# Queries and keys split in place, a mixer chunk tied behind attention, a late copy moved, and a last tile's low half written across partitions

## The chip, the cores and the metric

The kernel runs on one core of a Trainium2 chip, in one launch. The metric is device time in microseconds (us). The engines are TensorE (PE, with its weight loads as PEld), VectorE (DVE), ScalarE (ACT), GpSimd (POOL) and SyncE (SP), which issues most of the DMAs. Every engine runs its own instructions strictly in the order in which they stand.

## The reference, cut to what matters

Three stages follow each other, all in float32: attention with 4 batches of 8 heads, then a token-shift mixture, then an MLP mixer.

```python
def _attn_ref(q, k, v, s):                      # q, k, v: (4, 8, 576, 64)
    scores = scale * np.matmul(q, k.transpose(0, 1, 3, 2))
    cum = np.cumsum(np.maximum(s, 0.0), axis=-1)
    bias = -(cum[:, :, :, None] - cum[:, :, None, :])
    scores = np.where(causal, -1e9, scores + np.minimum(bias, 0.0))
    scores = scores - np.max(scores, axis=-1, keepdims=True)
    attn = np.exp(scores)
    attn = attn / (np.sum(attn, axis=-1, keepdims=True) + 1e-09)
    return np.matmul(attn, v)

def _moe_ref(x, mu_k, mu_r, w_k, w_v, w_r):     # x: (4, 576, 512), d_ff 1024
    xk = mu_k * x + (1.0 - mu_k) * x_prev
    xr = mu_r * x + (1.0 - mu_r) * x_prev
    k = np.maximum(xk @ w_k, 0.0)
    v = k * k @ w_v
    r = 1.0 / (1.0 + np.exp(-(xr @ w_r)))
    return r * v

def _moe2_ref(x, w_tok1, w_tok2, w_ch1, w_ch2): # d_tok 256, d_ch 1536
    h = np.maximum(x.transpose(0, 2, 1) @ w_tok1, 0.0) @ w_tok2
    u = x + h.transpose(0, 2, 1)
    return u + np.maximum(u @ w_ch1, 0.0) @ w_ch2
```

## The kernel before

Float32 products are made of pairs: each operand is split into a high part (rounded to a shorter format, F32R) and a low part (the rest), and a product is high by high, high by low and low by high. `products` (line 108) is the helper through which all matmuls of the two later stages go.

**Attention.** The rows of batch 0 are done first, with simpler operands ("early" and "late" items). Batches 1 to 3 are 24 visits, one head each, `i` = 0 to 23. A visit has a tile of 128 queries per item `j` = 0 to 3; an even visit has a fifth item, `j` = 4, for the last 64 queries of its own head and of the next one together. That makes 108 items (`items`). An item is one chain: score matmuls (`scores`, lines 307 and 308), a maximum on DVE (278), an exponential on ACT (289), a sum on POOL (290), a reciprocal on DVE (291), a normalisation on POOL (292), and then transposes on PE (435) and the product with the values (493).

**The operands of a visit.** `X1[i % 2]` and `X2[i % 2]` are four tiles in all, so the tiles of visit `i` are free for visit `i + 2` when its last score matmul (the pair item's, for an even visit) has run. `x1` holds the bias rows and the high parts, `x2` the high and low parts crossed. Before the change they come from DRAM: `load` brings a quarter of the raw queries and keys of two heads into the tile `PB`; `split` (lines 238 to 240) makes the high part by a copy on ACT, the low part by a subtraction on POOL, and stores both to the DRAM tensor `hl_d`; `place` (266 to 269) later reads them back by three DMAs, and the bias rows by a fourth. All those DMAs are issued by SP.

**The mixture's work as filler.** `moe_units` cuts the mixture of a batch into units of 12 matmuls (`up` makes `h`, `gate` makes `r`, half a `down` makes `vd`), 20 units for each of its two column chunks (256 and 320 columns). These units are spread between attention items by the table `starts, ends` (792) and the loop behind it. The second chunk of batch 0 is spread from item `base + 1` on, where `base` is the first of the 108 items.

**What sets the order.** A scheduler at build time orders each engine's instructions by priority, set with `at(place)`, and by when it reckons that an instruction could start. The kernel's written order is thus not the engines' order; the rows in the section on the change show that.

**The late copy.** `late_pv` (423) ends with a DVE copy of a head pair's product into the mixture's input `xt`.

**The token stage.** `y_transpose` (853 to 860) makes `YN`, transposed rows in high and low parts; for the last tile of 64 rows the low part is made in the low half's own place and a DMA (860) copies it to partitions 64 to 127, behind the high part. `tok1` multiplies both at once (872, 873).

Of the kernel before, what the change touches and what calls it, by code (L numbers as in the profile page):

```python
# [19 lines left out]
def f32(ap):  # L20
    return ap.bitcast(F32)
# [3 lines left out]
def attention_moe_mixer(  # L25
# [189 lines left out]

    qk_raw = {}

    def stage():
        if "PB" not in act:
            act["PB"] = qk_p.tile([128, 8 * QC], F32, tag="HX", name="PB")  # L220
        return act["PB"]

    def part(y):
        x, c = divmod(y, 2)
        return x, S * c // 2, S * (c + 1) // 2

    def load(i, y):
        g = visits[i][0]
# [43 lines left out]

    def softmax_max(j, ps, P, mx, x, c0, c1, mask=None):
        q0 = 128 * j
        m = 128 if mask is not None else min(128, S - 128 * j)
        if mask is None:
            mask = maskc[:, 512 - q0 + c0:512 - q0 + c1]
        nc.vector.tensor_tensor_reduce(  # L278
            out=P[0:m, c0:c1], in0=ps[0:m, 0:c1 - c0], in1=mask[0:m],
            scale=-scale, scalar=3.0e38 if x == 0 else mx[0:m, x - 1:x],  # L280
            op0=ALU.add, op1=ALU.min, accum_out=mx[0:m, x:x + 1],
        )

# [10 lines left out]
    def scores(i, j):  # L294
# [7 lines left out]
        for x, (c0, c1) in enumerate(parts):  # L302
            ps = ps_s.tile([128, 512], F32, tag="s", name="s")
            for e in (1, 0) if pair else (0,):
                x1, x2 = xs(i + e)
                n, a = (TAIL * (1 + e), S - TAIL * (1 + e)) if pair else (128, q0)
                nc.tensor.matmul(ps[0:n, 0:c1 - c0], x1[:, 0, a:a + n], x1[:, 1, c0:c1], start=True, stop=False)
                nc.tensor.matmul(ps[0:n, 0:c1 - c0], x2[:, 0, a:a + n], x2[:, 1, c0:c1], start=False, stop=True)
            softmax_max(j, ps, P, mx, x, c0, c1, None if not pair else maskp if x else maskc[:, 0:c1])
        softmax(j, P, mx, x, pair)  # L310
        pst[i, j] = P

# [69 lines left out]
    def late(h, j):  # L382
# [28 lines left out]
    def late_pv(h):  # L411
# [233 lines left out]
    def attention_item(n):  # L645
        if n < N1:
# [7 lines left out]
            if h >= H - 4:  # L654
                x = 3 * (h - H + 4) + j - 2
                with at(N0 + n + 0.1):
                    if x >= 4 and x < 8:
                        split(0, x - 4)
                    if x in (2, 3, 4, 5):
                        load(0, x - 2)  # L660
                    if x == 8:
                        load_v(0)
                    if x in (10, 11):
                        load(2, x - 10)
# [19 lines left out]
        if j == 0 and i + 1 < len(visits):  # L684
            with at(N0 + n):
                place(i + 1)
        if i % 2 == 0:
            with at(N0 + n + 0.1):
                if j < 4 and i + 2 < len(visits):
                    split(i + 2, j)  # L690
                    if j < 2:
                        load(i + 2, 2 + j)
                if j == NS - 1 and i + 2 < len(visits):
                    load_v(i + 2)
        else:
            with at(N0 + n + 0.1):
                if 2 <= j < 4 and i + 3 < len(visits):
                    load(i + 3, j - 2)
            if j == 1 and i + 1 < len(visits):
                with at(N0 + n + 0.2):  # L700
                    split_v(i + 1)
# [150 lines left out]
    def y_transpose(b, h):  # L852
        for i in range(NS):
# [170 lines left out]
```

## Time and profile before

| | us |
|---|---|
| three timed runs | 877.49, 1112.56, 873.9 (median 877.49) |
| the profiled execution | 872.61 |
| its span, first to last instruction | 870.8 |

The granted TensorE clock of the profiled execution is 0.992 of full speed on the mean. PE is busy 840.6 us of the span, its weight loads 790.5 us, DVE 485.1, ACT 452.6 and POOL 343.4. One timed run is far above the other two and is left out of everything that follows. "Busy" of PE is drawn from matmuls that overlap each other, so a PE that is busy throughout can still be slower than it could be.

### The profile page before, as it was taken

Reading aid. Unit: us, or ns where it says so; the run is one execution under the profiler, and the core shown is the slowest. Engines: PE = TensorE matmul, PEld = TensorE weight load, DVE = VectorE, ACT = ScalarE, POOL = GpSimd, SP = SyncE. Lnnn points to the kernel's source line nnn. Section 1 sums busy time; section 2 is a strip of 40 time slices with the busy share of each in tenths; the row PEclk is TensorE's granted clock in tenths of the full one; section 3 lists DMA queues with packets and bytes.
Section 4 is the critical chain, followed back from the end, with each engine's and each line's share of the span. In section 5 each row is a group of like instructions: output and inputs, shape, how many; then the busy total and the mean of one; then the engine's idle time right before and its main releaser. Section 6 shows DMA issues by size and latency. Waiting matters only on the chain. (4 is left out here: it accounts for less than half of the span.)

```text
span 870.8 us, 17455 instructions
## 1 busy us (share of the span) xinstructions
PE 840.6 (97%) x6127; PEld 790.5 (91%) x6127; DVE 485.1 (56%) x1352; ACT 452.6 (52%) x1257; POOL 343.4 (39%) x601
## 2 busy tenths in 40 slices
PE   8889998999899999999999999999999999999998
PEld 5656777988789999999999989999999999999998
DVE  5797776565879566985469757951331222222221
ACT  4688766865886656868377865840310221211210
POOL 4565666864785544645256854720000000000000
PEclk9899999999999999999999999999999999999999
DMA  7943778687974244431234746553021112112100
GB/s 191 266 134 88 199 218 230 192 240 210 252 204 133 70 111 117 100 93 41 83 94 129 230 143 217 177 181 94 7 92 54 44 31 74 42 32 73 38 25 26
DMA packets 88024, 108.36 MB, mean 124 GB/s; under 512 B 11152, under 2 KB 71568, under 8 KB 87936
## 3 DMA queue, kind: packets, MB, share of 16 engines
q1 hardware_dynamic: 81408, 91.56, 37.7%
q0 software_dynamic: 4576, 15.08, 5.5%
q8 instruction: 49, 0.80, 0.4%
q10 hardware_dynamic: 1952, 0.60, 0.3%
q14 instruction: 39, 0.32, 0.1%
HBM read 77.74 MB, written 28.90 MB: 122 GB/s over the span
## 5 line engine op out<-in xcount | busy, mean ns | idle before, releaser
L863 ACT ACTIVATE HID<-c 128x256 fp32r<-128x256 f32 (+1 forms) x96 | 39.3, 410 | 220.9 <-PE c L108 220.8
L108 PE MATMUL vd<-KK,WV 128*128 128x256 f32 (+1 forms) x768 | 120.9, 300 | 0.1
L108 PEld LDWEIGHTS vd<-KK,WV 128*128 128x128 f32 x768 | 106.6, 188 | 2.4 <-issue 0.9
L292 POOL TENSOR_SCALAR P<-P,sum 128x128 f32<-128x128 f32 (+4 forms) x148 | 93.6, 636 | 36.2 <-DVE sum L291 30.2
L108 PE MATMUL h<-XK,WK 128*128 128x320 f32 (+1 forms) x672 | 105.9, 303 | 0.7 <-DVE XK L517 0.5
L108 PE MATMUL c<-HID,WV 128*128 128x256 f32 (+1 forms) x768 | 104.9, 291 | 0.0
L108 PE MATMUL c<-U,WK 128*128 128x256 f32 (+1 forms) x768 | 103.2, 291 | 1.4 <-DVE HID L864 1.4
L289 ACT ACTIVATE P<-P,mx 128x128 f32<-128x128 f32 (+4 forms) x148 | 86.9, 588 | 30.3 <-DVE mx L278 23.0
L108 PEld LDWEIGHTS c<-HID,WV 128*128 128x128 f32 x768 | 100.6, 188 | 0.0
L108 PEld LDWEIGHTS c<-U,WK 128*128 128x128 f32 x768 | 98.6, 188 | 1.7 <-DVE HID L864 1.7
L108 PEld LDWEIGHTS h<-XK,WK 128*128 128x128 f32 x672 | 93.8, 189 | 2.1 <-DVE XK L517 0.7
L864 DVE SCALAR_TENSOR_TENSOR HID<-c,HID 128x256 fp32r<-128x256 f32 (+1 forms) x96 | 43.8, 456 | 81.1 <-ACT HID L863 81.0
L278 DVE CUSTOM_DVE_ANT_0 P<-s,maskc 128x128 f32<-128x128 f32 (+4 forms) x148 | 69.1, 478 | 22.1 <-PE t L435 8.4
L928 DVE TENSOR_TENSOR ut<-c,ut 128x256 f32<-128x256 f32 (+1 forms) x32 | 14.6, 458 | 119.3 <-PE c L108 112.0
L529 POOL TENSOR_TENSOR KK<-k,KK 128x256 fp32r<-128x256 f32 (+1 forms) x64 | 55.8, 877 | 19.8 <-ACT k L528 18.7
L108 PE MATMUL r<-XR,WR 128*128 128x320 f32 (+1 forms) x384 | 60.0, 299 | 0.0
L290 POOL TENSOR_SCALAR sum<-sum 128x1 f32<-128x1 f32 (+1 forms) x148 | 32.4, 219 | 67.6 <-ACT P L289 57.2
L108 PE MATMUL c<-HID,WR 128*128 128x256 f32 (+1 forms) x384 | 54.8, 291 | 0.0
L108 PEld LDWEIGHTS r<-XR,WR 128*128 128x128 f32 x384 | 52.8, 188 | 1.1 <-ACT raw L614 0.4
L108 PE MATMUL c<-U,C1A 128*128 128x256 f32 (+1 forms) x384 | 52.8, 296 | 0.1
L108 PEld LDWEIGHTS c<-U,C1A 128*128 128x128 f32 x384 | 51.5, 190 | 0.3 <-ACT U L913 0.3
L108 PEld LDWEIGHTS c<-HID,WR 128*128 128x128 f32 x384 | 51.3, 188 | 0.0
(133 smaller groups left out, 1658.4 us busy)
## 6 DMA issues: line engine op xcount, KB each, us to landing
X<-hl_d SPq DMA_DIRECT2D x72, 288.0 KB
hl_d<-PB SPq DMA_DIRECT2D x48, 288.0 KB
raw<-in_moe_w_ch_dram POOLq DMA_DIRECT2D x48, 256.0 KB, 3.3
PB<-in_qk_dram SPq DMA_DIRECT2D x48, 144.0 KB
yt<-y_d SPq DMA_DIRECT2D x16, 288.0 KB
u_d<-yt SPq DMA_DIRECT2D x16, 288.0 KB
raw<-in_moe_w_k_dram SPq DMA_DIRECT2D x8, 512.0 KB
raw<-in_moe_w_v_dram SPq DMA_DIRECT2D x16, 256.0 KB
```

Of the source, the lines that this page charges most:

```text
L108: nc.tensor.matmul(ps, a, b, start=first and i == 0, stop=last and i == n - 1)
L278: nc.vector.tensor_tensor_reduce(out=P[0:m, c0:c1], in0=ps[0:m, 0:c1 - c0], in1=mask[0:m], scale=-scale, scalar=3.0e38 if x == 0 else mx[0 ...
L289: nc.scalar.activation(out=P[0:m, 0:w], in_=P[0:m, 0:w], func=AF.Exp, bias=mx[0:m, x:x + 1], scale=-1.0, accum_out=sm[0:m, 0:1])
L290: nc.gpsimd.tensor_scalar(out=sm[0:m, 0:1], in0=sm[0:m, 0:1], scalar1=1e-9, scalar2=1.0, op0=ALU.add, op1=ALU.mult)
L292: nc.gpsimd.tensor_scalar(out=P[0:m, 0:w], in0=P[0:m, 0:w], scalar1=sm[0:m, 1:2], scalar2=1.0, op0=ALU.mult, op1=ALU.mult)
L529: nc.gpsimd.tensor_tensor(out=kk[:, 1, m, 0:n], in0=t[:, 0:n], in1=f32(kk[:, 0, m, 0:n]), op=ALU.subtract)
L863: nc.scalar.activation(out=hi, in_=ps, func=AF.Relu)
L864: nc.vector.scalar_tensor_tensor(out=lo, in0=ps, scalar=0.0, in1=f32(hi), op0=ALU.max, op1=ALU.subtract)
L928: nc.vector.tensor_tensor(out=t, in0=ps, in1=t, op=ALU.add)
```

## The change

Four edits:

1. Queries and keys are loaded raw, a head at a time, into one half of the partitions of a tile `RQ` (even visits in partitions 0 to 63, odd ones in 64 to 127), two visits ahead. When the operand tiles come free, `place` makes the high part by two copies on ACT straight into `x1`, the low part by four subtractions on POOL straight into `x2`, and copies the high part from `x1` to `x2` by two DMAs within the chip's own memory. `hl_d` and its stores and reads are gone.
2. The units of batch 0's second mixture chunk are spread over items `base + 3` to `base + PER + 8` (before: `base + 1` to `base + PER + 2`; `PER` is 36), and each is tied: its PE instructions stand behind the last score matmul of the item at which it is planned (`heads`). Batch 1's 40 units start 6 items later and end where they did.
3. The last late copy is issued behind the maximum of visit 0's second item.
4. The low part of `YN`'s last tile is written by DVE across partitions, without the DMA.

```diff
-    hl_d = dram.tile([G - H, D, 4, S], F32, name="hl_d")
...
-    def split(i, y):
-        g = visits[i][0] - H
-        x, c0, c1 = part(y)
-        t = qk_raw.pop((i, y))
-        e = stage()[:, S + y % 2 * S:S + y % 2 * S + S].rearrange("p (t s) -> p t s", t=2)
-        copy("A", e[:, 1].bitcast(F32R), t)
-        nc.gpsimd.tensor_tensor(out=e[:, 0], in0=t, in1=e[:, 1], op=ALU.subtract)
-        nc.sync.dma_start(out=hl_d[g:g + 2, :, 2 * x:2 * x + 2, c0:c1].rearrange("h d t s -> (h d) t s"), in_=e)
+    def sides(i):
+        a, z = slice(0, D), slice(D, 2 * D)
+        return (a, z) if i % 2 == 0 else (z, a)
...
+    def load(i):
+        nc.sync.dma_start(out=raw_qk()[sides(i)[0]], in_=qk[visits[i][0]])
...
     def place(i):
         g = visits[i][0]
-        t = hl_d[g - H]
         if i < 2:
             X2[i] = x_tile(2 + i, F32R)
         x1, x2 = xs(i)
-        nc.sync.dma_start(out=f32(x1[0:4]), in_=ext_d[g])
-        nc.sync.dma_start(out=f32(x1[64:128]), in_=t[:, 1:4:2])
-        nc.sync.dma_start(out=f32(x2[0:64]), in_=t[:, 0:4:3])
-        nc.sync.dma_start(out=f32(x2[64:128]), in_=t[:, 1:3])
+        a, z = sides(i)
+        rq = raw_qk()[a]
+        nc.sync.dma_start(out=f32(x1[z][0:4]), in_=ext_d[g])
+        for y in (1, 0):
+            nc.scalar.activation(out=x1[a, y], in_=rq[:, y], func=AF.Copy)
+            high, low = (z, a) if y else (a, z)
+            nc.sync.dma_start(out=f32(x2[high, y]), in_=f32(x1[a, y]))
+            for c in range(2):
+                cs = slice(S * c // 2, S * (c + 1) // 2)
+                nc.gpsimd.tensor_tensor(out=x2[low, y, cs], in0=rq[:, y, cs], in1=f32(x1[a, y, cs]), op=ALU.subtract)
+        if i + 2 < len(visits):
+            load(i + 2)
...
+    def last_late_copy():
+        with tc.issue_after(maxima[-1]):
+            copy("D", xt[0, H // 2 - 1][:, 1 + QC:1 + S], late_ps[H // 2 - 1])
...
-    starts, ends = [0, 2, 4, 4], [2, 4, 4, 4]
+    starts, ends = [0, 8, 4, 4], [8, 4, 4, 4]
...
-                m = base + 1
+                m = base + 3
                 todo.setdefault(m + (x1 - m) * x // len(u1), []).append(acts)
-            x1 = base + 1
+                tied.add(id(acts))
+            x1 = base + 3
...
-            with at(N0 + n + 3):
+            with at(N0 + n + 3), tc.issue_after(heads[n - 0]) if id(acts) in tied else ExitStack():
                 run(acts)
...
-            nc.vector.tensor_tensor(out=YN[0:r, 1, i, :], in0=ps[0:r, :], in1=f32(YN[0:r, 0, i, :]), op=ALU.subtract)
-        nc.sync.dma_start(out=f32(YN[TAIL:2 * TAIL, 0, NS - 1, :]), in_=f32(YN[0:TAIL, 1, NS - 1, :]))
+            low = YN[:, 1, i, :] if r == 128 else YN[TAIL:2 * TAIL, 0, i, :]
+            nc.vector.tensor_tensor(out=low, in0=ps[0:r, :], in1=f32(YN[0:r, 0, i, :]), op=ALU.subtract)
```

**PE, from the last items of visit 7 to the first transposes of visit 8.** `s` are scores (`X_1469` and `X_1471` are `x1` of even and odd visits, `X_1576` and `X_1718` their `x2`), `t` transposes of a normalised tile, `pv` products with the values, `h` and `vd` units of the mixture. `P_2948` is the last tile of visit 7 and `P_2987` the first of visit 8. Before:

```order
L307 MATMUL s<-X_1469 64x288
L308 MATMUL s<-X_1576 64x288
L435 MATMUL t<-ident,P_2948 128x128 x4
L493 MATMUL pv<-PF,VV_1933 128x256 x2
L493 MATMUL pv<-PF,VV_1933 128x128 x2
L435 MATMUL t<-ident,P_2987 128x128
L307 MATMUL s<-X_1471 128x128
L308 MATMUL s<-X_1718 128x128
L307 MATMUL s<-X_1471 128x256
L308 MATMUL s<-X_1718 128x256
```

After the change, where the same two tiles are `P_2866` and `P_2925`, and the odd visits' `x1` and `x2` are `X_1445` and `X_1659`:

```order
L434 MATMUL t<-ident,P_2866 128x128 x4
L107 MATMUL h<-XK,WK 128x256 x3
L492 MATMUL pv<-PF,VV_1902 128x256 x2
L492 MATMUL pv<-PF,VV_1902 128x128 x2
L300 MATMUL s<-X_1445 128x288
L301 MATMUL s<-X_1659 128x288
L300 MATMUL s<-X_1443 64x288
L301 MATMUL s<-X_1538 64x288
L434 MATMUL t<-ident,P_2925 128x128
L434 MATMUL t<-ident,P_2938 128x128 x2
L300 MATMUL s<-X_1445 128x128
L301 MATMUL s<-X_1659 128x128
L107 MATMUL vd<-KK,WV 128x320 x12
```

What moved: before, no unit of the mixture stands between the scores of visit 8's last items and those of visit 9 (nor, further on, until visit 10's second item); now a unit stands between most of them.

**POOL, while visit 4 is under way.** `P` are normalisations, `sum` the sums before them. Before, `PB` are subtractions of `split` for later visits:

```order
L292 TENSOR_SCALAR P_2376<-P_2376,sum 128x128
L290 TENSOR_SCALAR sum<-sum 128x1
L239 TENSOR_TENSOR PB<-PB 128x288
L290 TENSOR_SCALAR sum<-sum 128x1
L292 TENSOR_SCALAR P_2393<-P_2393,sum 128x256
L292 TENSOR_SCALAR P_2435<-P_2435,sum 128x384
L239 TENSOR_TENSOR PB<-PB 128x288
```

After, where `P_2342`, `P_2383` and `P_2400` are visit 4's tiles, and `X_1538` is `x2` of the even visits, being refilled for visit 6:

```order
L285 TENSOR_SCALAR P_2342<-P_2342,sum 128x256
L283 TENSOR_SCALAR sum<-sum 128x1
L285 TENSOR_SCALAR P_2383<-P_2383,sum 128x384
L283 TENSOR_SCALAR sum<-sum 128x1
L260 TENSOR_TENSOR X_1538<-RQ,X_1443 64x288 x3
L285 TENSOR_SCALAR P_2400<-P_2400,sum 128x512
L260 TENSOR_TENSOR X_1538<-RQ,X_1443 64x288
```

What moved: single subtractions scattered among the normalisations, done whenever their data were there, became four in a bunch, at the moment when the operand tile comes free.

## Rows read from the trace of the kernel before

**Rows 1.** The page: span, busy time, and weight loads in 40 slices.

```profile
span 870.8 us, 17455 instructions
...
PE 840.6 (97%) x6127; PEld 790.5 (91%) x6127; DVE 485.1 (56%) x1352; ACT 452.6 (52%) x1257; POOL 343.4 (39%) x601
...
PEld 5656777988789999999999989999999999999998
```

**Rows 2.** Windows of the attention stage: length, then engines' busy time, clock, DMA share.

```profile
137.00:150.00 13.00, 10.58 (x64) 8.75 (x63) 8.33 (x31) 8.81 (x26) 9.90 (x20) 0.93 0.92 239
150.00:214.00 64.00, 61.72 (x434) 59.49 (x433) 39.27 (x133) 45.80 (x128) 43.00 (x79) 0.99 0.78 216
214.00:262.00 48.00, 41.41 (x299) 37.03 (x298) 36.78 (x118) 38.73 (x115) 36.02 (x66) 1.00 0.82 225
262.00:300.00 38.00, 37.92 (x293) 36.89 (x292) 29.78 (x92) 26.14 (x72) 21.13 (x42) 1.00 0.40 111
300.00:437.00 137.00, 137.00 (x1036) 135.90 (x1034) 90.82 (x284) 89.30 (x242) 63.72 (x120) 1.00 0.35 91
```

**Rows 3.** Waits between 137 and 275 us: in total, times, longest.

```profile
ACT PB L75 <- DMA PB<-in_qk_dram: 22.8, 17, 3.6
POOL PB L239 <- ACT PB L75: 16.5, 12, 3.2
...
PE s L308 <- DMA X<-hl_d: 4.1, 3, 2.3
```

**Rows 4.** Timeline of ACT from 215 us.

```profile
216.08 0.45 ACT L75 ACTIVATE PB<-PB 128x288 fp32r<-128x288 f32 x1 [3.56 <-DMA PB<-in_qk_dram]
```

**Rows 5.** Timeline of PE from 224 us.

```profile
227.40 0.66 PE L493 MATMUL pv<-PF,VV 128*128 128x256 f32 x4
229.40 0.33 PE L435 MATMUL t<-ident,P 128*128 128x128 f32 x1 [1.34 <-POOL P L292]
```

**Rows 6.** Waits of PE between 150 and 214 us, the longest.

```profile
PE s L308 <- DMA X<-hl_d: 1.2, 1, 1.2
```

**Rows 7.** Groups of ACT by form: count, busy us, mean ns.

```profile
L289 ACT ACTIVATE P<-P,mx 128x576 f32<-128x576 f32 x12 | 9.3, 773 | 4.9 <-DVE mx L278 4.7
...
L289 ACT ACTIVATE P<-P,mx 64x576 f32<-64x576 f32 x8 | 6.3, 787 | 0.9 <-DVE sum L291 0.9
...
L75 ACT ACTIVATE PB<-PB 128x288 fp32r<-128x288 f32 x48 | 21.2, 441 | 30.7 <-DMA PB<-in_qk_dram 29.8 <-POOL PB L239 0.3 <-issue 0.2
...
L463 ACT ACTIVATE PT<-t 128x512 fp32r<-128x512 f32 x24 | 14.2, 594 | 0.5 <-PE t L435 0.2
```

**Rows 8.** Groups of POOL by form.

```profile
L239 POOL TENSOR_TENSOR PB<-PB 128x288 f32<-128x288 f32 x48 | 40.0, 835 | 23.9 <-ACT PB L75 18.6 <-DMA y_d<-e 3.7 <-DVE sum L291 0.6
...
L529 POOL TENSOR_TENSOR KK<-k,KK 128x320 fp32r<-128x320 f32 x32 | 29.4, 923 | 14.0 <-ACT k L528 13.8
...
L292 POOL TENSOR_SCALAR P<-P,sum 128x512 f32<-128x512 f32 x32 | 26.2, 820 | 12.6 <-DVE sum L291 11.0 <-PE t L435 1.0 <-PE h L108 0.4
```

**Rows 9.** Timeline of PE from 138 us: start, length.

```profile
138.20 0.29 PE L308 MATMUL s<-X 128*64 128x288 f32 x1
...
147.07 0.30 PE L308 MATMUL s<-X 128*128 128x128 f32 x1 [2.31 <-DMA X<-hl_d]
```

**Rows 10.** Timeline of SP from 139 us.

```profile
141.13 0.60 SPq L269 DMA_DIRECT2D X<-hl_d  x1
```

**Rows 11.** Timeline of PE from 470 us, a stretch without waits.

```profile
470.48 3.34 PE L108 MATMUL vd<-KK,WV 128*128 128x256 f32 x28
473.66 0.96 PE L108 MATMUL t<-T,H 128*128 128x288 f32 x6
...
476.24 3.68 PE L108 MATMUL h<-XK,WK 128*128 128x320 f32 x24
479.76 1.75 PE L108 MATMUL t<-T,H 128*128 128x288 f32 x12
```

**Rows 12.** The subtraction's line: shortest, median, longest in ns, first and last start.

```profile
L239 POOL TENSOR_TENSOR PB<-PB x48: 788/810/1083, 91.3 to 267.4; 128x288 f32<-128x288 f32 x48
```

**Rows 13.** PE's waits from 437 to 600 us.

```profile
PE c L108 <- DVE HID L864: 1.4, 1, 1.4
PE t L108 <- DVE yt L883: 1.2, 2, 1.0
PE t L872 <- DMA YN<-YN: 1.1, 1, 1.1
```

More of the change, by code (lines that the diff above doesn't have):

```diff
@@ L142, in attention_moe_mixer @@
     X1, X2, PT, VV = {}, {}, {}, {}
+    heads, maxima = [], []
     xt = {}
@@ L214, in xs, with raw_qk @@
         return X1[i % 2], X2[i % 2]
[L216 to L228, printed above, removed]
-        x, c0, c1 = part(y)
-        t = qk_raw[i, y] = stage()[:, y % 2 * S // 2:(y % 2 + 1) * S // 2]
-        nc.sync.dma_start(out=t, in_=qk[g:g + 2, :, x, c0:c1].rearrange("h d s -> (h d) s"))
-    def split(i, y):
-        g = visits[i][0] - H
-        x, c0, c1 = part(y)
-        t = qk_raw.pop((i, y))
-        e = stage()[:, S + y % 2 * S:S + y % 2 * S + S].rearrange("p (t s) -> p t s", t=2)
-        copy("A", e[:, 1].bitcast(F32R), t)
-        nc.gpsimd.tensor_tensor(out=e[:, 0], in0=t, in1=e[:, 1], op=ALU.subtract)
-        nc.sync.dma_start(out=hl_d[g:g + 2, :, 2 * x:2 * x + 2, c0:c1].rearrange("h d t s -> (h d) t s"), in_=e)
+    def sides(i):
+        a, z = slice(0, D), slice(D, 2 * D)
+        return (a, z) if i % 2 == 0 else (z, a)
+    def raw_qk():
+        if "RQ" not in act:
+            act["RQ"] = qk_p.tile([128, 8 * QC], F32, tag="HX", name="RQ")
+        return act["RQ"][:, 0:2 * S].rearrange("p (t s) -> p t s", t=2)
+    def load(i):
+        nc.sync.dma_start(out=raw_qk()[sides(i)[0]], in_=qk[visits[i][0]])
     def load_v(i):
@@ L277, in softmax_max @@
             mask = maskc[:, 512 - q0 + c0:512 - q0 + c1]
-        nc.vector.tensor_tensor_reduce(
+        maxima.append(nc.vector.tensor_tensor_reduce(
             out=P[0:m, c0:c1], in0=ps[0:m, 0:c1 - c0], in1=mask[0:m],
@@ L281, in softmax_max @@
             op0=ALU.add, op1=ALU.min, accum_out=mx[0:m, x:x + 1],
-        )
+        ).ins)
     def softmax(j, P, mx, x, pair=False):
@@ L307, in scores @@
                 nc.tensor.matmul(ps[0:n, 0:c1 - c0], x1[:, 0, a:a + n], x1[:, 1, c0:c1], start=True, stop=False)
-                nc.tensor.matmul(ps[0:n, 0:c1 - c0], x2[:, 0, a:a + n], x2[:, 1, c0:c1], start=False, stop=True)
+                mm = nc.tensor.matmul(ps[0:n, 0:c1 - c0], x2[:, 0, a:a + n], x2[:, 1, c0:c1], start=False, stop=True)
             softmax_max(j, ps, P, mx, x, c0, c1, None if not pair else maskp if x else maskc[:, 0:c1])
         softmax(j, P, mx, x, pair)
+        heads.append(mm.ins)
         pst[i, j] = P
@@ L391, in late @@
             ps = ps_s.tile([128, 512], F32, tag="s", name="s")
-            nc.tensor.matmul(ps[0:m, 0:c1 - c0], x[0:D + 4, 0, q0:q0 + m], x[0:D + 4, 1, c0:c1], start=True, stop=True)
+            mm = nc.tensor.matmul(ps[0:m, 0:c1 - c0], x[0:D + 4, 0, q0:q0 + m], x[0:D + 4, 1, c0:c1], start=True, stop=True)
             softmax_max(j, ps, P, mx, y, c0, c1)
+        heads.append(mm.ins)
         softmax(j, P, mx, y)
@@ L421, in late_pv @@
             nc.tensor.matmul(pv[rs, o:CM], late_v[p][0:r, k, rs], T[0:r, BLK[k] + o:BLK[k] + CM], start=k == 0, stop=k == NS - 1)
-        if e == 1:
+        if e == 1 and h < H - 1:
             copy("D", xt[0, p][:, 1 + QC:1 + S], pv)
+    def last_late_copy():
+        with tc.issue_after(maxima[-1]):
+            copy("D", xt[0, H // 2 - 1][:, 1 + QC:1 + S], late_ps[H // 2 - 1])
     def transposes(i, j):
@@ L653, in attention_item @@
                     late_values(h // 2 + 1)
-            if h >= H - 4:
-                x = 3 * (h - H + 4) + j - 2
+            if h == H - 3 and j == 2:
                 with at(N0 + n + 0.1):
[L657 to L664, printed above, removed]
+                    load(0)
+                    load(1)
+            if h == H - 2 and j == 4:
+                with at(N0 + n + 0.1):
+                    load_v(0)
             if h == H - 1 and j == 3:
@@ L686, in attention_item @@
                 place(i + 1)
-        if i % 2 == 0:
+        if i % 2 == 0 and j == NS - 1 and i + 2 < len(visits):
             with at(N0 + n + 0.1):
[L689 to L701, printed above, removed]
+                load_v(i + 2)
+        if i % 2 and j == 1 and i + 1 < len(visits):
+            with at(N0 + n + 0.2):
+                split_v(i + 1)
         with at(N0 + n):
             scores(i, j)
+        if (i, j) == (0, 1):
+            with at(N0 + n - 0.5):
+                last_late_copy()
         with at(N0 + n + 1.5):
@@ L791, in attention_moe_mixer @@
     base = (NS - 2) * H
-    starts, ends = [0, 2, 4, 4], [2, 4, 4, 4]
+    starts, ends = [0, 8, 4, 4], [8, 4, 4, 4]
+    tied = set()
     for b in range(B):
```

2 lines of the change are left out of this document (1 added, 1 removed).

## Prediction

> **What bounds the kernel now.** I read the page first: PE is busy 840.6 of 870.8 us, so nothing but its own waits can be won, and the slices of its weight loads show where these are, ahead of slice 14 or so of 40 [rows 1]. The first 100 us hold many of them, but the order on PE up to there is the same after the change. Then I read the windows of the attention stage [rows 2]. From 300 to 437 us weight loads run 135.90 of 137 us: 1.1 us lost, 0.8%. From 137 to 262 us they run 8.75 of 13, 59.49 of 64 and 37.03 of 48 us: 4.25, 4.51 and 10.97, together 19.73 us lost; from 262 to 300 it is 1.11. Next the waits of that stretch. Only 4.1 us of PE's own are on a DMA of the operands [rows 3]. More telling is ACT: 17 times the copy of `split` at the head of its queue waits for a raw quarter still on its way, 22.8 us in all, and everything behind it waits along. One of these, 3.56 us up to 216.08 [rows 4], lies at the start of the poorest stretch. The first transpose of visit 8 then finds its tile not ready and PE stands 1.34 us at 229.40 [rows 5], with no unit of the mixture in between, as the order shows: units were run as soon as PE had room, and are used up where the chains come late.
>
> **A rule on how to count.** By PE's matmul row the loss from 137 to 262 us is 2.42 + 2.28 + 6.59 = 11.3 us, by the weight loads 19.7 [rows 2]. The matmul counts side with the second: 299 in 48 us against 1036 in 137 is 160 ns against 132 each, and 299 at 132 ns would be 39.5 us, 8.5 less than they took, where the matmul row shows 6.6 idle. The Trainium skill ("Trainium Kernel Development and Optimization", Performance Expectations) says that matmul busy time is a bad metric because matmuls are pipelined, and that the busy share of the weight loads is a good one. By the matmul row the ceiling of the first term below would be 8.4 us lower.
>
> **The change part by part.**
>
> *The round trip through DRAM goes.* 48 stores to `hl_d`, 72 reads from it and 48 quarter loads leave SP's queue; 24 loads and 48 short copies come. The raw head is now loaded two visits ahead, so ACT's 22.8 us of waits for it [rows 3] go. ACT's and POOL's own work grows: per visit two copies of 64x576 and four subtractions of 64x288 stand for two and two of 128x288. Half the partitions save nothing: the exponential takes 787 ns on 64 partitions and 773 on 128 [rows 7]. A copy of 576 columns is not in the trace; from below 594 ns (512 columns), from above 787 ns; I take 0.66, since 128x512 is the nearest and 288 to 512 columns cost 441 to 594 ns, 0.7 ns a column [rows 7]. A subtraction is 0.835 us [rows 8], so a visit has 1.3 us of ACT (0.9 before) and 3.3 us of POOL (1.7 before).
>
> *What that costs while PE waits for it.* The refill of `x1` and `x2` starts when the tile's last score matmul has run. Its chain is: ACT finishes what it holds (0 to 3 instructions, about 0.6 us each), 0.66 copy, four subtractions 3.3, and on POOL one or two strangers in between, a normalisation 0.82 and a unit's subtraction 0.92 [rows 8]. That is 4.0 us at least, 7.5 at most without a wait, and I take 7.0, since the order shows such strangers within the bunch. The two copies by DMA run beside the subtractions. Before, the same path (free at 138.49 and used at 147.07 [rows 9], last read issued at 141.13 [rows 10]) took 8.6 us with the DMA engines 92% taken [rows 2]. How long PE has other work meanwhile I count in the new order and price at 0.114 us for a matmul of 256 columns (28 from 470.48 to 473.66) and 0.147 for 320 (24 from 476.24 to 479.76) [rows 11], 0.11 for a transpose: for the even visits 2 to 22 it is 6.3, 8.9, 6.7, 8.4, 6.7, 5.9, 8.9, 7.8, 8.3, 6.0 and 10.9 us; odd visits have 7.6 and more. For visit 6 that is 24 units' matmuls 3.5, nine value products 1.1, six transposes 0.7 and eight score matmuls of 128 to 512 columns 1.3. A chain of 7.0 us comes late by 0.7 + 0.3 + 0.3 + 1.1 + 1.0 = **+3.4 us**. At 4.0 us it is 0, at 9 us 16.
>
> *The tie and the new spread.* It adds and removes no work; it holds 20 units back so that one stands behind each second item or so. Priced as above, the work on PE between an item's scores and its transposes was 5.0 to 9.2 us in visits 7 and 8; in the new order the same items have 9.8 to 12.3, and the poorest afterwards is 5.9. What remains then? The stretch 150 to 214 us has such filler now, with POOL at 67% and ACT at 72%; without its wait for operands (1.2 us [rows 6]) it loses 3.3 of 64 us, 5.2% [rows 2]. At 5.2% the 125 us from 137 lose 6.5 instead of 19.7: **-13.2 us**. At the 0.8% of 300 to 437 it would be -18.7; if only half comes back, -7. The 2.31 us stop at 147 was followed by a slower clock, 0.93 of full over 13 us and 0.99 over 64 [rows 2]: 0.9 + 0.6 = **-1.5 us** if the stop goes; if it does not, 0.
>
> *The price of moving load.* `split` was done by 268 us for all visits [rows 12], so the stretch from 300 to 437 us had none of it. Now 11 visits there add 36 us to POOL's 63.7 of 137 (73%) and 14 to ACT's 89.3 (76%), and batch 1's units are squeezed into 32 items from 38. That is a little fuller than they are in 150 to 214 us. I take a loss of 3.0%, halfway between 0.8 and 5.2: **+3.0 us**; the ends are 0 and 8.5 (7%, what 150 to 214 us lose with their wait).
>
> *A rule against the change.* The 48 subtractions took 0.788 to 1.083 us [rows 12]; something slows some of them. The Trainium skill ("SBUF — State Buffer", Who interferes with whom) says that a DVE instruction with two inputs from this memory contends with a GpSimd instruction that reads it. With every subtraction at 1.083, as an estimate by that page, the chain would be 1.0 us longer and the sum about 5 us more; the median of those seen is 0.810, so I leave it.
>
> *The low half across partitions.* Eight DMAs go and none comes; DVE's instructions stay as many. One of them shows as a wait of PE, 1.1 us [rows 13]: **-1.1 us**. Below, 0, if another wait takes its place (the neighbours of 1.2 and 1.4 us are on DVE [rows 13]).
>
> *The late copy* is one DVE instruction of some 0.5 us that no longer stands ahead of two maxima. It feeds the fourth block of the mixture's input, and the new order gives PE three blocks' worth of two units first: 0, and 1 us either way.
>
> The sum, on the profiled execution's own time: 872.6 - 13.2 - 1.5 - 1.1 + 3.0 + 3.4 = **863.2 us**, said as 863. The undisturbed timed runs lie 1.3 and 4.9 us above the profiled one, which the range has to hold.
>
> **Rivals.**
> *The stretch fills up wholly*, as 300 to 437 us does now, with no late refill: -18.7 - 1.5 - 1.1, **851 us**. For it: the ACT waits of 22.8 us vanish outright. Against: four engines are over 65% busy there.
> *The load only moves:* the gain halves to -7 and the dense stretch loses the full 8.5 at 7%: **872 us**, no change. For it: POOL's share there rises from 47 to 73%.
> *The refill becomes the bound (slower).* The copies now wait at the head of ACT's queue for PE's last score matmul, and exponentials queue behind them; the four subtractions then hold POOL 3.3 us; and SP's store of the mixture's result, which waits for a `down`, can stand ahead of the refill's DMAs. If the chain takes 10.5 us, even visits come late by 4.2, 1.6, 3.8, 2.1, 3.8, 4.6, 1.6, 2.7, 2.2 and 4.5, 31 us in all, and the time is 863.2 - 3.4 + 31 = **891 us**; 2% slower is 890, so it decides from 10.5 us on. For it: 8.6 us was seen before. Against: that path had four DMAs at 92% load in it, this one has two short ones off the path.
> *The tie does little* because PE's order was already right for most items: only the DMA waits (4.1 [rows 3]), the clock's drop and `YN` go: 872.6 - 4.1 - 1.5 - 1.1 + 3.0 = **869 us**.
>
> **How the numbers follow.** Forecast (857 to 868 us) 0.52, filled wholly 0.20, load only moves or tie does little 0.21, refill bound 0.07. Two per cent, which is about what a measurement of this kernel can tell from no change, is 855 us on the profiled scale: faster holds the filled case and 0.06 of the forecast's lower edge, 0.26; slower is the refill case, 0.07; within 2% is the rest, 0.67. The range goes from the filled case to beyond the moved load with the timed runs' offset: 850 to 877.
>
> **What would show it.** Right: no wait of ACT for a raw load; weight loads above 93% from 137 to 262 us, no clock drop near 148, filler between visits 8 and 10, no wait of `tok1` on a DMA. Wrong: PE's score matmuls waiting for POOL's `x2` at even visits, by more than 5 us in all; weight loads below 95% from 300 to 437 us.

## The result, and the profile after

The changed kernel takes 885.94 us (median of 6 runs, 884.28 to 887.91) against 875.41 us for the kernel before (median of five; a sixth, at 1112.56 us, is left out). The ratio is 1.0123, with a 95% interval of 1.0107 to 1.014. The forecast was 863, which is 1.1% faster on the scale of the profiled execution; the kernel came out 1.2% slower, 9 us above the range. The profiled execution took 885.16 us, its span 883.4: 12.6 more than before [rows 1].

The page of the changed kernel, with span, busy time and weight loads in 40 slices:

```profile
span 883.4 us, 17408 instructions
...
PE 845.5 (96%) x6127; PEld 793.8 (90%) x6127; DVE 500.1 (57%) x1352; ACT 464.9 (53%) x1257; POOL 381.2 (43%) x649
...
PEld 5656677889888999989989899899999999999998
```

PE does the same 6127 matmuls. DVE, with the same 1352 instructions, is busy 15 us longer; POOL 38 us, ACT 12. The windows of the changed kernel in the stages of [rows 2], and those that follow:

```profile
137.00:150.00 13.00, 10.83 (x66) 9.06 (x65) 9.57 (x29) 8.80 (x22) 11.01 (x16) 0.94 0.44 103
150.00:214.00 64.00, 59.12 (x399) 55.98 (x400) 40.07 (x140) 48.46 (x127) 48.85 (x91) 0.96 0.28 70
214.00:262.00 48.00, 46.31 (x354) 43.68 (x353) 37.93 (x113) 38.92 (x105) 37.53 (x65) 1.00 0.30 76
262.00:300.00 38.00, 34.84 (x256) 33.87 (x257) 27.89 (x86) 25.09 (x67) 27.99 (x48) 0.96 0.29 76
300.00:437.00 137.00, 133.35 (x999) 130.69 (x999) 99.52 (x286) 97.49 (x258) 89.32 (x153) 1.00 0.21 55
437.00:490.00 53.00, 50.70 (x405) 50.49 (x404) 37.07 (x82) 32.58 (x92) 24.05 (x35) 0.97 0.36 113
490.00:562.00 72.00, 68.32 (x471) 66.31 (x469) 52.04 (x105) 49.72 (x144) 44.45 (x66) 1.00 0.61 193
...
562.00:883.40 321.40, 315.61 (x2467) 314.60 (x2465) 96.84 (x224) 68.71 (x188) 19.23 (x28) 1.00 0.21 63
```

The last three of the kernel before:

```profile
437.00:490.00 53.00, 52.87 (x432) 52.26 (x430) 42.31 (x95) 41.05 (x119) 36.26 (x48) 1.00 0.41 128
490.00:562.00 72.00, 67.33 (x461) 65.47 (x462) 53.28 (x114) 50.33 (x147) 43.18 (x65) 1.00 0.60 188
...
562.00:870.80 308.80, 305.37 (x2397) 305.00 (x2395) 83.86 (x196) 56.95 (x153) 9.27 (x14) 1.00 0.20 60
```

Length less weight loads is the loss of a stage. The poorest stage did improve, 214 to 262 us from 10.97 to 4.32 us. But 150 to 214 went from 4.51 to 8.02, 262 to 300 from 1.11 to 4.13, 300 to 437 from 1.10 to 6.31, 437 to 490 from 0.74 to 2.51, and the end from 3.80 to 6.80, with 490 to 562 and 137 to 150 a little better: 8.7 us more from 137 us on. Weight loads themselves are 3.3 us longer by the page, and there the clock shows.

These windows are fixed in time, so the late ones don't hold the same work in both kernels: the last has 2465 weight loads against 2395. The count of matmuls gives a fairer scale, that is, when the n-th of the 6127 starts in either trace. By it the changed kernel is 7.6 us behind at the 2900th, when attention is over. At the 3000th it is 11.6 behind, by a single stop at 461 us and the slow clock after it; at the 3950th 12.7, and from there on it loses nothing more.

The longest waits of PE from 137 to 600 us in the changed kernel:

```profile
PE s L300 <- DVE mx L271: 4.0, 3, 2.2
PE t L107 <- ACT YN L849: 2.3, 1, 2.3
PE t L107 <- ACT k L525: 2.3, 1, 2.3
PE pv L492 <- ACT PT L452: 1.9, 3, 0.8
PE t L434 <- POOL P L285: 1.8, 2, 1.2
...
PE t L434 <- POOL VV L244: 1.4, 1, 1.4
```

Every wait on a DMA of [rows 3] and [rows 13] is gone, and so are ACT's 22.8 us for raw quarters. In their place PE waits for links of the softmax's chain, on all three other engines. One such place, on POOL and then on PE, at the end of visit 4:

```profile
191.81 1.02 POOL L244 TENSOR_TENSOR VV<-VS,VV 128x384 fp32r<-128x384 f32 x1
192.90 2.45 POOL L260 TENSOR_TENSOR X<-RQ,X 64x288 fp32r<-64x288 f32 x3
195.46 0.74 POOL L285 TENSOR_SCALAR P<-P,sum 128x576 f32<-128x576 f32 x1
196.28 0.79 POOL L260 TENSOR_TENSOR X<-RQ,X 64x288 fp32r<-64x288 f32 x1
197.18 0.37 POOL L285 TENSOR_SCALAR P<-P,sum 128x128 f32<-128x128 f32 x1
```

```profile
196.26 0.66 PE L434 MATMUL t<-ident,P 128*128 128x128 f32 x4 [1.23 <-POOL P L285]
...
197.60 0.41 PE L492 MATMUL pv<-PT,VV 128*128 128x320 f32 x1 [0.58 <-ACT PT L452]
199.50 2.40 PE L492 MATMUL pv<-PT,VV 128*128 128x320 f32 x9 [1.49 <-DVE PT L453]
```

Three subtractions of the new split stand ahead of the normalisation of the visit's last item (195.46), which PE has waited for; its copies and values come late in turn. Three such clusters of stops were followed by 3.4 us at half the granted clock that the kernel before has not; these windows hold two of them:

```profile
199.60:203.00 3.40, 3.40 (x17) 3.40 (x17) 0.86 (x5) 0.40 (x1) 0.40 (x1) 0.50 0.00 0
267.80:271.20 3.40, 3.40 (x17) 3.40 (x18) 3.34 (x11) 0.00 (x0) 1.65 (x5) 0.51 0.49 130
```

The granted clock is half there, 1.2 instead of 2.4 GHz, and the engine shows as busy throughout. Three such spells (the third runs from 462.4 to 465.8 us) cost at most 3 x 1.7 = 5.1 us, an estimate from these rows; the weight loads grew by 3.3.

To see the chain as a whole I took, for each item that starts between 140 and 445 us (102 of them), the time from the end of its last score matmul to the end of its normalisation in the trace. The mean went from 7.45 to 10.12 us: 1.36 more up to the exponential, 0.99 more from its end through POOL's step on the sum to DVE's reciprocal, 0.32 more for the normalisation's turn.

### The profile page after: what moved, and what is told of

It is laid out like the page before. It is cut to its first block, busy times and chain, and to the rows that moved or that the text cites. A ratio compares the mean times of both kernels' runs of the same rounds, so it can differ in the third digit from the quotient of the medians.

```text
span 883.4 us, 17408 instructions
## 1 busy us (share of the span) xinstructions
PE 845.5 (96%) x6127; PEld 793.8 (90%) x6127; DVE 500.1 (57%) x1352; ACT 464.9 (53%) x1257; POOL 381.2 (43%) x649
## 4 chain that ended last, share of the span: by engine, by line
PE 70%; DVE 9%; ACT 8%; DMA 5%; POOL 4%; issue 3%; SPq 0%; ACTq 0%; DVEq 0%; POOLq 0%
PE c L107 32%; PE vd L107 8%; PE h L107 7%; PE r L107 4%; PE t L107 3%; PE pv L492 3%; PE t L434 2%; PE s L386 2%; PE pv L416 2%; DMA raw<-in_moe_w_ch_dram 2%; PE s L300 2%; POOL X L260 1%; PE s L301 1%; ACT P L282 1%; DMA VV<-in_v_dram 1%
## 5 line engine op out<-in xcount | busy, mean ns | idle before, releaser
L285 POOL TENSOR_SCALAR P<-P,sum 128x128 f32<-128x128 f32 (+4 forms) x148 | 95.4, 648 | 41.6 <-DVE sum L284 32.1
L260 POOL TENSOR_TENSOR X<-RQ,X 64x288 fp32r<-64x288 f32 x96 | 78.9, 838 | 8.8 <-ACT X L255 4.9
L528 POOL TENSOR_TENSOR KK<-k,KK 128x256 fp32r<-128x256 f32 (+1 forms) x64 | 52.3, 823 | 20.6 <-ACT k L527 19.2
```

The lines of the kernel that those rows point to most:

```text
L260: nc.gpsimd.tensor_tensor(out=x2[low, y, cs], in0=rq[:, y, cs], in1=f32(x1[a, y, cs]), op=ALU.subtract)
L285: nc.gpsimd.tensor_scalar(out=P[0:m, 0:w], in0=P[0:m, 0:w], scalar1=sm[0:m, 1:2], scalar2=1.0, op0=ALU.mult, op1=ALU.mult)
L528: nc.gpsimd.tensor_tensor(out=kk[:, 1, m, 0:n], in0=t[:, 0:n], in1=f32(kk[:, 0, m, 0:n]), op=ALU.subtract)
```

## The experiments

All ratios are to the kernel before on the same chip, with their 95% interval.

**One edit at a time.** e1_split_alone puts edit 1 on the kernel before, the core of which is

```
+            nc.scalar.activation(out=x1[a, y], in_=rq[:, y], func=AF.Copy)
+            nc.sync.dma_start(out=f32(x2[high, y]), in_=f32(x1[a, y]))
+            for c in range(2):
+                nc.gpsimd.tensor_tensor(out=x2[low, y, cs], in0=rq[:, y, cs], in1=f32(x1[a, y, cs]), op=ALU.subtract)
```

> Edit 1 alone on the kernel before: queries and keys split in place, with the old table for the dense units, the old late copy and the old YN tile. Theory A (the split is the loss: four POOL subtractions of 0.838 us a visit come ahead of the last items' normalisations, TensorE stops for POOL and the clock drops after it): slower than before, ratio 1.008 to 1.018, with TensorE waits on POOL P or VV of 5 us or more in all. Theory B (the tie and its tighter table are the loss): ratio 0.985 to 1.000, since the 22.8 us of ScalarE waits for raw quarters are gone. Theory C (the re-planned order is the loss and no edit is it by itself): within 0.6% of before.

e2_tie_alone:

```
+    starts, ends = [0, 8, 4, 4], [8, 4, 4, 4]
+                m = base + 3
+            with at(N0 + n + 3), tc.issue_after(heads[n - 0]) if id(acts) in tied else ExitStack():
```

> Edit 2 alone on the kernel before: batch 0's second chunk tied behind the scores of its item, spread from the third item on over 41 instead of 37 items, and batch 1's units over 32 instead of 38. Theory A: 0.992 to 1.000, since nothing of it loads POOL. Theory B: 1.008 to 1.018, with the weight loads of 300 to 437 us below 97% as after the whole change. Theory C: within 0.6% of before.

e4_low_tile_alone:

```
+            low = YN[:, 1, i, :] if r == 128 else YN[TAIL:2 * TAIL, 0, i, :]
-        nc.sync.dma_start(out=f32(YN[TAIL:2 * TAIL, 0, NS - 1, :]), in_=f32(YN[0:TAIL, 1, NS - 1, :]))
```

> Edit 4 alone on the kernel before: the low half of YN's last tile is written across partitions, without the DMA. All theories: 0.997 to 1.001, the 1.1 us wait on YN's DMA gone. A ratio further off than that would speak for theory C, as the order of all engines is planned anew.

m1_old_split is edits 2, 3 and 4 without edit 1 (the rest of the diff).

> Edits 2, 3 and 4 on the kernel before, the split left as it was (through DRAM). Theory A: 0.985 to 1.000, no TensorE wait on POOL above 2 us. Theory B: 1.008 to 1.015. Theory C: within 0.6% of before, while the whole change is at 1.012.

Measured: e1 1.014 (1.0123 to 1.0156), e2 0.9974 (0.9956 to 0.9993), e4 1.0012 (0.9994 to 1.003), m1 0.9995 (0.9971 to 1.0019). The split is the whole loss; the other three edits together change nothing that can be told, and the tie alone gains 0.3% (at most 0.4%). Theory B falls by e2 and m1, theory C, as it was put, by e1. The waits did not take the form A named: PE stood 2.7 us for POOL and 6.1 for DVE's maxima in e1. Part of e1's loss, 3.9 us, falls between the 2950th and the 3000th matmul, in the same stop after attention as in the whole change (4.2 us).

These are the windows of m1, without the split in place:

```profile
137.00:150.00 13.00, 11.92 (x76) 9.50 (x73) 9.59 (x32) 7.75 (x22) 9.30 (x17) 1.00 0.92 232
150.00:214.00 64.00, 60.15 (x426) 57.54 (x425) 42.98 (x145) 49.14 (x139) 48.61 (x90) 1.00 0.89 242
214.00:262.00 48.00, 42.27 (x305) 41.28 (x306) 37.26 (x111) 37.66 (x109) 34.84 (x61) 0.89 0.81 227
...
300.00:437.00 137.00, 137.00 (x1034) 135.81 (x1033) 91.16 (x280) 88.57 (x240) 60.70 (x117) 1.00 0.35 92
```

From 137 to 262 us m1 loses 16.7 us, e2 16.4, where the kernel before loses 19.7: the tie and its spread by themselves win at most 3 us there. By the count of matmuls, which takes in the slow clock, m1 and e2 are only 0.8 and 1.5 us ahead at the 1550th.

**Which part of the split.** c1_no_subs and c2_no_copies leave work out, c3_subs_on_dve and c4_spread move it:

```
c1  -                nc.gpsimd.tensor_tensor(out=x2[low, y, cs], ...)
c2  +            if i < 2:
                     nc.scalar.activation(out=x1[a, y], in_=rq[:, y], func=AF.Copy)
c3  +                nc.vector.tensor_tensor(out=x2[low, y, cs], ...)
c4  +        if j == 2 and i + 1 < len(visits):
    +            with at(N0 + n):
    +                place(i + 1, (0,))
```

> The changed kernel without the 96 POOL subtractions of the split: the low halves of queries and keys are left out (set to zero once), all else as changed. It prices 80.5 us of POOL work. Theory A1 (POOL is the loss: VectorE's operations with two operands in SBUF run longer beside it, 868 against 540 ns at the mixer's blend, and normalisations stand behind it): ratio to before 0.980 to 0.992, VectorE's blends back near before, no stop of TensorE above 2 us after 150 us. Theory A3 (ScalarE's copies, held for X and ahead of exponentials, are the loss): 1.005 to 1.014, as the copies stay. Theory A4 (the dense stage after attention loses by itself, by the order planned for it): 1.003 to 1.008.

> The changed kernel with ScalarE's copies of queries and keys left out from the third visit on (44 of 48; the scores then use old high halves), subtractions kept. It prices about 30 us of ScalarE and what waits behind it. Theory A1: 1.006 to 1.014, the loss stays. Theory A3: 0.985 to 1.000.

> The changed kernel with the 96 subtractions on VectorE in place of POOL, the whole result computed. VectorE gets about 96 x 0.36 = 35 us and loses the slowing beside POOL (about 11 us). Theory A1: 0.985 to 1.003, faster than the change by 1% or more. If VectorE becomes the bound in 214 to 262 us, where it was busy for 79%: 1.005 to 1.02. Theory A3: 1.008 to 1.015.

> The changed kernel with a visit's refill in two parts: keys at the first item of the visit before, queries at its third; the same instructions otherwise. Theory A2 (the bunch of four subtractions ahead of the normalisations is the loss, not their sum): 0.990 to 1.003. Theory A1 (their sum and what they slow): 1.007 to 1.015.

Measured: c1 0.9849 (0.9818 to 0.988), c2 1.0014 (0.9992 to 1.0036), c3 1.014 (1.0105 to 1.0174), c4 1.015 (1.0111 to 1.0188). Against the change's 1.0123 the subtractions price at 2.7% of the time, the copies at 1.1%. c1 came out as A1 has it, DVE's blends included (562 and 569 ns), but for one stop of 2.3 us at 543 us. c2 lies between the two ranges, so A3 has a share too; without the copies the subtractions can also start sooner, and how much of the 1.1% that is stays open. Spreading (A2) gives nothing. c3 missed A1's range: on DVE a subtraction takes 505 ns, 45 us in all and not 35, and PE waits for maxima instead, 7.3 us. So POOL is not the only engine on which this work costs time; DVE, which makes the maxima of the same chain, is another. The windows of c1_no_subs in four stages of the attention:

```profile
137.00:150.00 13.00, 11.59 (x74) 9.20 (x72) 9.73 (x30) 9.16 (x23) 5.80 (x13) 1.00 0.52 129
150.00:214.00 64.00, 63.43 (x462) 61.98 (x463) 46.26 (x156) 52.71 (x142) 34.59 (x73) 1.00 0.34 82
214.00:262.00 48.00, 47.36 (x387) 46.61 (x385) 43.46 (x142) 42.19 (x115) 26.62 (x55) 1.00 0.31 76
...
300.00:437.00 137.00, 136.85 (x1046) 134.90 (x1046) 91.07 (x271) 92.75 (x256) 61.31 (x114) 1.00 0.24 66
```

Here the stretch from 150 to 262 us fills as the forecast wanted: 2.0 and 1.4 us are lost, with POOL at 54 and 55% instead of 76 and 78. The scores still need the copy and the transfer of the refill.

**POOL's load, wherever it comes from.** k1_lead gives the chain more look-ahead, k2_dummy_pool loads POOL in the kernel before, k3_stage splits on 128 partitions in a staging tile and moves the result into place by DMA:

```
k1  -        with at(N0 + n + 1.5):
    +        with at(N0 + n + 2):
                 transposes(i, j)
k2  +                for _ in range(2):
    +                    nc.gpsimd.tensor_tensor(out=spare[:, 0], in0=spare[:, 0], in1=f32(xs(i)[0][0:64, 1, 0:S // 2]), op=ALU.subtract)
k3  +        nc.scalar.activation(out=rq[:, 1].bitcast(F32R), in_=rq[:, 0], func=AF.Copy)
    +            nc.gpsimd.tensor_tensor(out=rq[:, 2, cs].bitcast(F32R), in0=rq[:, 0, cs], in1=rq[:, 1, cs], op=ALU.subtract)
    +            nc.sync.dma_start(out=f32(x1[a, y]), in_=hi)
    +            nc.sync.dma_start(out=f32(x2[high, y]), in_=hi)
    +            nc.sync.dma_start(out=f32(x2[low, y]), in_=lo)
```

> The changed kernel with transposes half an item later (2.0 instead of 1.5 items behind the scores, values at 2.5): more look-ahead for the softmax chain, the same work. From scores to normalised tile takes 10.1 us on the mean there against 7.45 us before. Theory L (the longer chain is no longer covered by the look-ahead): 0.990 to 1.005. Theory T (the sum of work on the three in-order vector engines is what paces the stage): 1.007 to 1.017, as the change.

> The kernel before, its split through DRAM kept, with 46 more POOL subtractions of 64x288 that nobody waits for (two at the start of each visit): POOL's load is that of the changed kernel (about 38 us more). Theory P (POOL's load, wherever it comes from, delays sums and normalisations and slows VectorE): 1.006 to 1.016. Theory I (it is the in-place refill itself, copy and subtraction ahead of the next visit's scores): 0.997 to 1.004.

> The changed kernel with the split on 128 partitions: queries in the lower, keys in the upper half of one staging tile, one copy of 128x576 and two subtractions of 128x288 a visit, and six transfers from there into place, none through DRAM. POOL then has 48 subtractions of 0.834 us (40 us) instead of 96 (80 us), ScalarE 24 copies instead of 48. Theory P: 0.982 to 0.997, between the kernel before and the one without subtractions. Theory I: 1.000 to 1.015, since copy, subtraction and a transfer of about 2 us stand ahead of the next visit's scores.

Measured: k1 1.0094 (1.0075 to 1.0112), k2 1.012 (1.0105 to 1.0135), k3 0.9962 (0.9944 to 0.9979). k2 is the test: 46 subtractions that nobody waits for,

```profile
L690 POOL TENSOR_TENSOR spare<-spare,X 64x288 f32<-64x288 f32 x46 | 37.9, 823 | 14.5 <-DMA X<-ext_d 12.5 <-DVE mx L280 0.7
```

cost the kernel before as much as the change costs. So POOL's load is enough by itself, without the new split's place. k2 is not a clean test of the way, though: its subtractions held POOL's queue for 12.5 us more, until the DMAs of the tile that they read had landed, and they stand in one queue with the old split's own subtractions: PE waits 7.0 us for the reads of `hl_d` (4.1 before). n3 below is cleaner on both counts. k3 agrees: with 48 subtractions instead of 96 the same idea is faster than before. k1 came out as theory T has it, but it isn't a fair test of L: the mean time from scores to transposes was 13.5 us there against 13.9 in the change, so the later place in the order gave no more look-ahead. k1 also lacks the change's stop at 461 us.

**By which way.** n1, n2 and n4 leave out POOL's step between exponential and reciprocal; n3_dummy_memset adds POOL work that only writes:

```
n1, n2, n4  -        nc.gpsimd.tensor_scalar(out=sm[0:m, 0:1], in0=sm[0:m, 0:1], scalar1=1e-9, scalar2=1.0, op0=ALU.add, op1=ALU.mult)
n3          +                with tc.issue_after(norms[-2]):
            +                    for _ in range(4):
            +                        nc.gpsimd.memset(spare, 0.0)
```

> The staged split on 128 partitions, and besides the softmax's sum goes from ScalarE straight to VectorE's reciprocal, without POOL's step in between (140 operations of 0.22 us, 31 us of POOL) that adds 1e-9 to a sum that is at least 1; that addition is left out and changes no digit of a sum of this size. Theory Q (sums and normalisations queue behind POOL's other work, and this is how POOL's load costs time): 0.975 to 0.989. Theory V (POOL costs by slowing VectorE alone): 0.992 to 0.998, as without the edit.

> The changed kernel with POOL's step on the sum left out in the same way. It keeps the 96 subtractions. Theory Q: 0.990 to 1.002, at least half of the loss back. Theory V: 1.008 to 1.014, since the subtractions beside VectorE stay.

> The kernel before with 92 POOL memsets of 64x448 that nobody waits for, four a visit, each put behind a normalisation (about 0.42 us each by the 64x1152 one of 1.06 us, 38 us in all). They only write, so they occupy POOL's queue as the 46 subtractions of the earlier run did. If VectorE's blends stay near 0.64 and 0.57 us: theory Q says 1.006 to 1.014, theory V 0.997 to 1.003. If the blends grow as they did there, the run doesn't tell the two apart.

> The kernel before with POOL's step on the sum left out. Theory Q: 0.985 to 0.995. Theory V: 0.997 to 1.002.

Measured: n1 0.9905 (0.9889 to 0.9921), n2 0.998 (0.9962 to 0.9997), n3 1.0126 (1.0097 to 1.0155), n4 1.0036 (1.0016 to 1.0056). n1 lies between the two ranges. n2 speaks for Q: all of the loss is back while the 96 subtractions stay and DVE's blends stay long (it also takes 31 us off POOL's queue, which is the same theory). By the count used above, its chain takes 7.8 us on the mean, against 10.1 in the change. These are the blends in the changed kernel, in n2 and in n3, by form with mean ns:

```profile
L514 DVE SCALAR_TENSOR_TENSOR t<-xt,omu,t 128x320 f32<-128x320 f32 x32 | 23.5, 747 | 0.1
...
L514 DVE SCALAR_TENSOR_TENSOR t<-xt,omu,t 128x256 f32<-128x256 f32 x32 | 20.5, 644 | 0.4
```

```profile
L513 DVE SCALAR_TENSOR_TENSOR t<-xt,omu,t 128x320 f32<-128x320 f32 x32 | 21.6, 691 | 0.1
L513 DVE SCALAR_TENSOR_TENSOR t<-xt,omu,t 128x256 f32<-128x256 f32 x32 | 21.1, 658 | 0.3
```

```profile
L517 DVE SCALAR_TENSOR_TENSOR t<-xt,omu,t 128x320 f32<-128x320 f32 x32 | 20.1, 642 | 0.2
L517 DVE SCALAR_TENSOR_TENSOR t<-xt,omu,t 128x256 f32<-128x256 f32 x32 | 18.5, 582 | 0.3
```

Before they took 638 and 568 ns. In n3 they are back near that and the kernel is as slow as the change: for Q again, though not cleanly, since the scaling ahead of the blend grew there by 5 us in all. Its memsets took longer than the 0.42 us that I had reckoned,

```profile
L691 POOL MEMSET spare<- 64x448 f32 x92 | 43.1, 469 | 1.7
```

but they wait for next to nothing, and PE waits only 2.0 us for the reads of `hl_d`; the chain takes 8.8 us on the mean, as in k2. c3's chain is as short as n2's, 7.9 us, and c3 is slow all the same, so the time up to the normalisation isn't all that counts.

At the 2900th matmul, when attention is over, the runs stand to the kernel before as follows: c1 -15.0 us, n1 -10.9, k3 -6.7, n2 -3.5, c3 +6.9, the change +7.6, k2 +12.4, n3 +13.9. So whether a run gains or loses is settled in attention, ahead of the stops that come later.

n4 contradicts the range that I gave Q: on the kernel before, the step's removal shortened the chain from 7.45 to 5.78 us and gave nothing. Its waits say why, on PE and on ACT:

```profile
PE s L307 <- DMA X<-hl_d: 7.9, 5, 2.2
```

```profile
ACT PB L75 <- DMA PB<-in_qk_dram: 29.5, 22, 4.8
```

There the split's transfers end last (4.1 us on PE in [rows 3]), and a faster chain only waits longer for them. The chain limits from some POOL load on, not below it.

**The version that beats both.** n1 is the staged split with that step left out. Its page and windows:

```profile
span 864.0 us, 17377 instructions
...
PE 840.8 (97%) x6127; PEld 793.3 (92%) x6127; DVE 486.3 (56%) x1352; ACT 449.6 (52%) x1233; POOL 306.7 (35%) x453
```

```profile
150.00:214.00 64.00, 63.40 (x456) 61.31 (x455) 45.32 (x154) 48.38 (x135) 38.96 (x57) 1.00 0.62 153
214.00:262.00 48.00, 45.57 (x365) 44.31 (x364) 42.83 (x133) 37.89 (x107) 29.53 (x43) 1.00 0.51 128
...
300.00:437.00 137.00, 136.28 (x1037) 134.35 (x1035) 92.64 (x272) 88.78 (x243) 60.55 (x87) 1.00 0.35 93
```

Two more on it: n5_old_table takes the tie and the late copy back (`starts, ends = [0, 2, 4, 4], [2, 4, 4, 4]`, `m = base + 1`), n6_stage_lead repeats k1's edit.

> The staged split without POOL's step on the sum (0.9905), with the old table of the dense units and the old late copy: edits 2 and 3 taken back. Whether the tie is worth anything where the split no longer loads POOL: if it is (the filler between items 137 to 262 us), 0.993 to 1.000; if not, 0.988 to 0.993.

> The staged split without POOL's step on the sum, and transposes half an item later. Theory L (the chain still limits): 0.980 to 0.987. If the chain of 6.4 us is covered by the look-ahead already: 0.988 to 0.993.

Measured: n5 0.9905 (0.9883 to 0.9928) and n6 0.9941 (0.9919 to 0.9964). The tie is worth nothing here either. n6 is just above both of its ranges: transposes half an item later are no better, rather worse. But as in k1 the transposes did not come later in fact (11.3 us behind the scores in n6 and in n1), so L has no run that tests it.

## Why the prediction was wrong, point by point

- **What bounds.** The reading was right that PE's waits are all there is to win, and that raw loads and transfers made the worst of them: all of these went. Wrong was to take the stretch's remaining loss for a constant, whatever is put on POOL.
- **The term of -13.2 is the step that failed.** It put the loss left in 137 to 262 us at 5.2%, the level of 150 to 214 us before, where POOL stood at 67%. It measured 16.28 us of 125, 13.0%, a gain of 3.4. POOL was at 76 and 78% there from 150 us on; with the subtractions out, c1 lost 7.2 us of the same 125, close to the 6.5 forecast. I had counted 3.3 us of POOL a visit against 1.7 and used that number for the refill's own chain and for the dense stage, but not for this stretch and its softmax, which passes POOL's queue twice an item. The term was also booked to the tie, which by e2 and m1 is worth at most 3 us of it. The rest needed the trip through DRAM gone without the load on POOL: c1 is 15.2 us ahead at the 1550th matmul, the changed kernel 1.0.
- **The dense stage, +3.0:** the mechanism was right, the size was not: 5.2 us more lost from 300 to 437, within the end of 8.5. The premises were off: 32 subtractions, 8 visits and not 11, fell there, and POOL stood at 65% and not 73. The moved load also costs 3.0 us in 262 to 300, which had no term. That the tighter table made it is excluded: m1 has the table, and its weight loads run 135.81 of 137 us there, 135.90 before.
- **The refill, +3.4:** its parts measured as priced (copy 674 ns for 0.66, subtraction 838 for 0.835), but PE's scores never waited for `x2`: 0. The rival built on it (891 us) had the sign for a wrong reason: not who waits for the four subtractions, but what stands behind them.
- **The clock, -1.5:** the stop at 147 us is still there with another cause (2.2 us on DVE's maxima), and three more slow spells came.
- **`YN`, -1.1:** the wait went, the time did not (1.0012 alone): 0, the lower end; waits on ACT stand in its place. The late copy wasn't tried alone: with the old table the mixer would read the block before it is written.
- **After attention,** 3.9 us more were lost from 437 us on, for which there was no term. The order planned at build differs there, and PE stopped twice for 2.3 us behind ACT. One stop, at 461 us and shown below, costs 4.2 us by the count of matmuls, a third of the whole loss; e1 and c3 have it too, k1, k2 and n3 do not. The other kind, on `YN`, is there without the split in place too (m1). How much of this belongs to the split stays open.
- **The rule weighed and left out** (DVE beside GpSimd) does act, but on DVE, which is 15 us longer, and not on the subtractions, at 838 ns on the mean. By n2 it is not what attention's time hangs on; the stop at 461 us has it at its head, and no run tests that.
- **The signs** would not have told: weight loads from 300 to 437 us ran 95.4% (wrong was below 95), and no score matmul waited for `x2`. Of the signs of being right two failed: 87% and not 93 from 137 to 262 us, and the clock's drop at 148.
- **The sum** of what was measured: -3.4 (137 to 262 us) + 3.0 + 5.2 (262 to 437) + 3.9 (after) + 3.3 (longer weight loads) + 0.5 (ahead of 137) is the 12.6 us of the two spans, within rounding.
- **The chances:** no rival was "the moved work lengthens a chain that does not use it", though the rows for it were there: POOL's normalisation and ACT's exponential stand in every item.

## What to carry to other kernels

When work moves onto an in-order engine, ask first which chain passes that engine's queue, and how often, and only then who waits for the work itself; a neutral test is to put as much work that nobody waits for on the same engine. Half the partitions cost the same time (a POOL subtraction of 288 columns took 838 ns on 64 partitions, 835 on 128): splitting two operands on 64 partitions each doubles the engine's load, and staging both on 128 and moving them by DMA gives it back. A small step on another engine inside a chain (here 0.22 us of POOL) costs its turn in that queue, but taking it out only pays where the chain is what ends last (n2 against n4). And look at all engines of the chain: the same work on DVE cost as much.

## What the runs showed of the hardware

An operation of DVE that takes its operands from SBUF can wait for POOL; the maxima, which read PSUM, did not. In the changed kernel the 128x320 blend took 540 ns on the mean of 9 with hardly any POOL work beside it, and 1042 ns (535 to 2207; two of them were not slowed) on the mean of 10 beside a POOL subtraction; the maxima of 128x512 took 683 ns in either kernel. The dearest case is at 457 us, on DVE, POOL, ACT and PE in turn:

```profile
457.29 1.59 DVE L516 TENSOR_TENSOR XR<-t,XR 128x256 fp32r<-128x256 f32 x1 [0.48 <-ACT XR L515]
...
460.27 0.42 DVE L516 TENSOR_TENSOR XR<-t,XR 128x256 fp32r<-128x256 f32 x1 [0.48 <-ACT XR L515]
```

```profile
457.15 1.44 POOL L528 TENSOR_TENSOR KK<-k,KK 128x256 fp32r<-128x256 f32 x2
```

```profile
459.82 0.42 ACT L515 ACTIVATE XR<-t 128x256 fp32r<-128x256 f32 x1 [2.26 <-DVE t L514]
```

```profile
461.23 0.98 PE L107 MATMUL t<-YN,T 128*128 128x256 f32 x6 [2.30 <-ACT k L525]
```

The subtraction that takes 0.42 us at 460.27 takes 1.59 at 457.29 and ends 0.3 us after POOL's pair (457.15 + 1.44). DVE's next blend is late, ACT's copy of it waits at the head of its queue, the unit's first copy stands behind that, and PE stops for 2.3 us and runs at half clock from 462.4 to 465.8. The Trainium skill ("SBUF — State Buffer", Who interferes with whom) says that the two engines share a pair of ports under an exclusive lock, so that the later one waits for the whole instruction of the other. The rows agree as far as they go: DVE's subtraction started 0.14 us behind POOL's and ended behind it. It waited out both instructions of the pair, not one.
